# A spectral filter beside a gated feed-forward network on one core: the DRAM scratch of its two turns split by sides, the filters read once and copied within SBUF, and unpadded filter rows

## The chip, the core and the metric

The kernel runs on one core of a Trainium2 chip. The metric is device time in microseconds (us) of one execution; the kernel before takes 204.1 us, the median of three runs (203.77 to 204.25).

The core's engines are TensorE (PE, with its weight loads shown as PEld), VectorE (DVE), ScalarE (ACT), GpSimd (POOL) and SyncE (SP), which here issues every transfer. SBUF is the on-chip memory of 128 partitions, PSUM the memory that TensorE writes.

## The reference, cut to what matters

```python
x = A_x                                    # (1, 2048, 640) bf16
xn = layernorm(x)                          # over the last axis, no scale
X = rfft2(xn.astype(float32))              # over (2048, 640): 2048 x 321 complex
s = irfft2(X * (w_r + 1j * w_i), s=(2048, 640)).astype(bfloat16)
h = (gelu(xn @ w_gate) * (xn @ w_up)) @ w_down    # 640 -> 1536 -> 640, tanh gelu
return x + s * silu(h)
```

`w_r` and `w_i` are 2048 x 321 filters in bf16. Two things are computed from the same normalized rows, then: a two-dimensional spectral filter and a gated feed-forward network.

## The kernel before, in words

**Slabs.** The 2048 rows are split as (n2, n1): slab n1 holds the rows 16 n2 + n1, 128 rows on 128 partitions, and there are 16 slabs (NS = 16). X holds all of them in SBUF.

**The feed-forward network** is the body of the work. For each of four groups of four slabs (g), `ffn_piece` (L714) multiplies the transposed rows xnT by the gate weights into a PSUM bank psg and by the up weights into psu; ACT evicts psg through GELU into ge (L718), and VectorE multiplies psu by ge into uT (L720). `down_third` (L738) then multiplies uT by the down weights, and ACT and VectorE make the silu factor G (L743, L746, L747). psg and psu have two PSUM buffers each.

**The spectral filter** is woven into this. It has these steps:
1. `fold_a`, `fold_b`: sums and differences of the rows' halves (VectorE).
2. `slab_S1`: the 128-point transform of a slab over n2, five matmuls into a PSUM tile pz (L484), which ACT copies into `zbuf` (L486).
3. `group_D`: the transform over the 640 columns for slab 0 alone and then for five groups of three slabs (DF), matmuls into two PSUM tiles pd (L494, L498). ACT, for two halves VectorE, copies them into `zdbuf` (L510), and SP stores them to the DRAM tile ZDR (L512), one transfer for each slab.
4. `load_B2` reads ZDR back with the 16 slabs on partitions (ten transfers, L530): the first turn.
5. `s2_in` and `s2_out`: in eleven bursts the 16-point transform over the slabs (px, L556), its copy xs (ACT, L564), its products with the filters W1 and W2 (VectorE, L568), the way back (pu, L583), its copies (ACT, L589), and stores to the DRAM tile UDR (L592).
6. `load_V` reads UDR back with rows on partitions (ten transfers, L603): the second turn. `gather` (VectorE, L613) collects leftover columns of V into vr.
7. `slab_S1i` (pv, L631; the fifth of its matmuls takes vr), `group_Di` and `group_cs`, `group_Y`: the inverse transforms; `finish` multiplies by G, adds x and stores.

pz, pd, px, pu and pv all come from one PSUM pool, `psB`, with two buffers under one tag.

**GEN.** One SBUF tile, GEN, is cut by hand into scratch. `vt` (index tables) becomes `zdbuf`, two slots for the groups of step 3, and `fv` (angles) becomes `zbuf`, four slots for the slabs of step 2:

```python
zbuf = fv.rearrange("p g l -> p (g l)").bitcast(BF16)[:, 0:4 * D]...
zdbuf = vt.rearrange("p n k -> p (n k)").bitcast(BF16)[:, 0:12 * LP]...
```

The two don't share bytes.

**The filters** lie in W1 and W2 with the partition index 64 hh + 4 k1 + 2 ri + pm. `w_rows` loads them from DRAM; the rows for ri = 0 and ri = 1 are the same, and are read twice, in rows of 321 values (642 B). `w_edge` (POOL, L127) halves the first and last column.

**What sets the order.** A list `back` names the network's pieces in order, and `put(s, ...)` hangs every other step behind piece s; the program is written out in that order, and each engine works its own instructions in order. For groups 1 to 5 the plan puts three slabs' `slab_S1` behind three successive pieces, `group_D` behind the next, and the next group's first `slab_S1` two pieces later. SP works its transfers in order too; a transfer that waits holds up all behind it. Eight semaphores are used by the transfers in turn, and a transfer waits until the eighth before it has landed. All other waits follow from which tiles an instruction reads and writes.

Of the kernel before, what the change touches and what calls it, by code (L numbers as in the profile page):

```python
# [10 lines left out]
BF16 = mybir.dt.bfloat16  # L11
# [3 lines left out]
P = 128  # L15
S = 2048
D = 640
L = 321
LP = 322
# [4 lines left out]
NS = 16  # L24
# [6 lines left out]
@with_exitstack  # L31
def kernel(
    ctx: ExitStack,
    tc: tile.TileContext,
    A_x: bass.AP,
    A_w_r: bass.AP,
    A_w_i: bass.AP,
    B_x: bass.AP,
    B_w_gate: bass.AP,
    B_w_up: bass.AP,  # L40
    B_w_down: bass.AP,
    out: bass.AP,
):

    nc = tc.nc
    x2 = A_x[0]
    xv = x2.rearrange("(n2 n1) d -> n2 n1 d", n1=NS)
    outv = out[0].rearrange("(n2 n1) d -> n1 n2 d", n1=NS)  # L50

    consts = ctx.enter_context(tc.tile_pool(name="consts", bufs=1))
    big = ctx.enter_context(tc.tile_pool(name="big", bufs=1))
    wts = ctx.enter_context(tc.tile_pool(name="wts", bufs=1))
    xg = ctx.enter_context(tc.tile_pool(name="xg", bufs=5))
    work = ctx.enter_context(tc.tile_pool(name="work", bufs=2))
    psA = ctx.enter_context(tc.tile_pool(name="psA", bufs=2, space=bass.MemoryType.PSUM))
    psB = ctx.enter_context(tc.tile_pool(name="psB", bufs=2, space=bass.MemoryType.PSUM))
    dram = ctx.enter_context(tc.tile_pool(name="dscratch", bufs=1, space=bass.MemoryType.DRAM))

    ZDR = dram.tile([2, NS, P, L], BF16)
    UDR = dram.tile([2, NS, P, L], BF16)


    X = big.tile([P, NS, D], BF16, tag="sX")
    Wg = wts.tile([P, 5, F], BF16)
    Wu = wts.tile([P, 5, F], BF16)
    Wd = wts.tile([P, NT, D], BF16)
    W1 = wts.tile([P, 2, NS, LP], BF16)
    W2 = wts.tile([P, 2, NS, LP], BF16)  # L70
    wgv = B_w_gate.rearrange("(c p) f -> p c f", p=P)
    wuv = B_w_up.rearrange("(c p) f -> p c f", p=P)
    with tc.manual_schedule():
        build(nc, locals())


def build(nc, env):
    consts, big, wts, xg, work, psA, psB = (env[k] for k in ("consts", "big", "wts", "xg", "work", "psA", "psB"))
    ZDR, UDR, X, Wg, Wu, Wd, W1, W2 = (env[k] for k in ("ZDR", "UDR", "X", "Wg", "Wu", "Wd", "W1", "W2"))
    xv, outv, wgv, wuv = (env[k] for k in ("xv", "outv", "wgv", "wuv"))  # L80
# [28 lines left out]

    spw = [(WT, src.rearrange("(k1 r) l -> k1 r l", k1=NS)) for WT, src in ((W1, A_w_r), (W2, A_w_i))]  # L110

    def w_rows(i, hh, ri, pm):
        WT, sp = spw[i]
        p0 = hh * 64 + ri * 2 + pm
        for lo in range(2):
            u0 = lo * 32 + hh * 16
            if pm == 0:
                nc.sync.dma_start(out=WT[p0:p0 + 61:4, lo, :, 0:L], in_=sp[:, u0:u0 + 16, :])
            elif u0 == 0:
                nc.sync.dma_start(out=WT[p0:p0 + 61:4, lo, 1:NS, 0:L], in_=sp[:, 127:112:-1, :])  # L120
                nc.sync.dma_start(out=WT[p0:p0 + 61:4, lo, 0, 0:L], in_=sp[:, 64, :])
            else:
                nc.sync.dma_start(out=WT[p0:p0 + 61:4, lo, :, 0:L], in_=sp[:, 128 - u0:112 - u0:-1, :])

    def w_edge(i):
        WT = spw[i][0]
# [30 lines left out]
    def c1(name, dt=FP32):  # L157
        return consts.tile([P, 1], dt, name=name)
# [64 lines left out]
    def bits(name, fields):  # L223
        n = len(fields)
        ti = consts.tile([P, n], INT32, name=name + "i")
        tf = consts.tile([P, n], FP32, name=name)
        for k, (shift, mask) in enumerate(fields):
            nc.vector.tensor_scalar(out=ti[:, k:k + 1], in0=pint, scalar1=shift, scalar2=mask,
                                    op0=ALU.logical_shift_right, op1=ALU.bitwise_and)
        nc.vector.tensor_copy(out=tf, in_=ti)  # L230
        return [tf[:, k:k + 1] for k in range(n)]

    def affine(name, src, a, b):
# [1 line left out]
        nc.vector.tensor_scalar(out=t, in0=src, scalar1=float(a), scalar2=float(b), op0=ALU.mult, op1=ALU.add)  # L235
        return t

    u_f, hi_f, s_f, h_f, pf, n1_f, z_f = bits(
        "pb", [(0, 63), (6, 1), (0, 31), (5, 1), (0, 127), (1, 15), (0, 1)])
    cs_f = h_f  # L240
    e64 = c1("e64")
    nc.vector.tensor_single_scalar(out=e64, in_=pf, scalar=64.0, op=ALU.is_equal)

    def fma(name, src, k, add, dt=FP32):
        t = c1(name, dt)
        nc.vector.scalar_tensor_tensor(out=t, in0=src, scalar=float(k), in1=add, op0=ALU.mult, op1=ALU.add)
        return t
# [3 lines left out]
    nc.vector.tensor_scalar(out=andm, in0=e64, scalar1=-1023.0, scalar2=2047.0, op0=ALU.mult, op1=ALU.add)  # L251
    orm = c1("orm", INT32)
    nc.vector.tensor_scalar(out=orm, in0=e64, scalar1=512.0, scalar2=None, op0=ALU.mult)
    u64 = fma("u64", e64, 64.0, u_f)

    def times(name, src, k, by):
        t = c1(name)
# [246 lines left out]
    def group_D(i):  # L504
        n0, n = DF[i]
        pd = d_group([Zt.pop(n0 + a) for a in range(n)], FT, LH)
        zd = zdbuf[:, i % 2, 0:n]
        for b in range(2):
            ev = nc.vector.tensor_copy if i in (2, 5) and b == 1 else nc.scalar.copy
            ev(out=zd.rearrange("p a c (m b) -> p a c m b", b=2)[:, :, :, :, b], in_=pd[b])  # L510
        for a in range(n):
            nc.sync.dma_start(out=ZDR[:, n0 + a].rearrange("c p l -> p c l"), in_=zd[:, a, :, 0:L])  # L512

    warm_bank = []

# [7 lines left out]

    def load_B2():
        B2 = big.tile([P, NH, L], BF16, tag="sB", name="B2")
        zv = ZDR.rearrange("c n (z a k h) l -> a (c n z) k h l", z=2, a=2, k=2)
        B4 = B2.rearrange("p (k h) l -> p k h l", k=2)
        for h0, h1 in ((0, 3), (3, 6), (6, 9), (9, 12), (12, 16)):
            for lo in range(2):
                nc.sync.dma_start(out=B4[64 * lo:64 * lo + 64, :, h0:h1, :], in_=zv[lo][:, :, h0:h1, :])  # L530
        st_b["B2"] = B2
        sc = X[:, 0:13, :].rearrange("p n d -> p (n d)")
        n_u, n_p = 2 * 3 * L, 2 * 3 * WB
        st_b["p"] = sc[:, 0:4 * n_p].rearrange("p (s q k x) -> p s q k x", s=2, q=2, k=2)
        st_b["u"] = sc[:, 4 * n_p:4 * n_p + 2 * n_u].rearrange("p (s k x) -> p s k x", s=2, k=2)
# [11 lines left out]
    def s2_in(b):  # L547
# [17 lines left out]
        pp = []  # L565
        for q, WT in enumerate((W1, W2)):
            pp.append(wide(st_b["p"][:, b % 2, q]))
            nc.vector.tensor_tensor(out=pp[-1], in0=xs, in1=WT[:, :, h0:h0 + n, l0:l0 + w], op=ALU.mult)  # L568
        st_b[b] = pp

    uv = UDR.rearrange("c n (z a k h) l -> a (c n z) k h l", z=2, a=2, k=2)

    def s2_out(b):
        h0, n, l0, w = BURSTS[b]
        pp = st_b.pop(b)
        pu = psB.tile([P, 2, 512], FP32, tag="b")
        for q, NM in enumerate((N1, N2)):
            for hh in range(2):
                r = slice(64 * hh, 64 * hh + 64)
                for lo in range(2):  # L580
                    for i, j, kind in s2_tiles(b, lo, hh):
                        ps = pu[64 * lo:64 * lo + 64, hh, i * w:j * w].rearrange("p (h l) -> p h l", l=w)
                        nc.tensor.matmul(ps, lhsT=NM[r, kind, 0:64], rhs=pp[q][r, lo, i:j, :],  # L583
                                         start=(q == 0 and i == 0), stop=(q == 1 and j == n))
        us = st_b["u"][:, h0 // 3 % 2, :, 0:n * L].rearrange("p k (h l) -> p k h l", l=L)
        pv = pu[:, :, 0:n * w].rearrange("p k (h l) -> p k h l", l=w)
        for m in range(2):
            c0 = m * LH + l0 // 2
            nc.scalar.copy(out=us[:, :, :, c0:c0 + (w + 1 - m) // 2], in_=pv[:, :, :, m:w:2])  # L589
        if l0 + w == L:  # L590
            for lo in range(2):
                nc.sync.dma_start(out=uv[lo][:, :, h0:h0 + n, :], in_=us[64 * lo:64 * lo + 64, :, :, :])  # L592

    st_c = {}

# [3 lines left out]
    def load_V():  # L599
        V = big.tile([P, NS, 2 * L], BF16, tag="sB", name="Vin")  # L600
        for n0, n in VP:
            for c in range(2):
                nc.sync.dma_start(out=V[:, n0:n0 + n, c * L:c * L + L],  # L603
                                  in_=UDR[c].rearrange("n p l -> p n l")[:, n0:n0 + n, :])
        st_c["V"] = V
        st_c["Y"] = big.tile([P, NS, D], BF16, tag="sX", name="Yall")

# [31 lines left out]

    w1f = W1.rearrange("p k n l -> p (k n l)")  # L640
    vsbuf = w1f[:, 0:4 * D].rearrange("p (s c k) -> p s c k", s=4, c=5)
# [153 lines left out]
    def put(s, *item):  # L795
        plan[s].append(item)
# [57 lines left out]
    for i, (n0, n) in enumerate(DF):  # L854
        a = F0 if i == 0 else F0 + 5 * i - 3
# [8 lines left out]
    for k in range(4):  # L864
        put(32 + 3 * k, slab_T, 8 + k, 2)
        put(65 + 3 * k, slab_T, 12 + k, 2)
    for k in range(16):
        put(8 + k if k < 8 else (32, 35, 38, 41, 44, 44, 47, 47)[k - 8], w_rows, k // 8, k % 8 // 4, k % 2, k % 4 // 2)
    put(40, w_edge, 0)
    put(z_end + 4, w_edge, 1)  # L870
    put(z_end, load_B2)
# [14 lines left out]
    for i, (n0, n) in enumerate(DG):  # L886
        a = vs0 + 15 * i // 2
# [58 lines left out]
```

## Time and profile before

| | |
|---|---|
| median of three runs | 204.1 us (203.77 to 204.25) |
| the profiled execution, whole | 204.42 us |
| its span | 202.6 us, 4209 instructions |
| PE, PEld busy | 195.6 us (97%), 119.8 us (59%) |
| DVE, ACT, POOL busy | 129.3 us (64%), 122.4 us (60%), 33.4 us (16%) |
| granted TensorE clock | 1.0 |
| transfers | 31.77 MB in 43315 packets, 157 GB/s on average |
| packets under 2 KB | 41504 |
| store to ZDR, issue to landing (median) | 5.3 us, 16 of 160.5 KB |
| loads of V, issue to landing (median) | 6.3 us, 6 of 321 KB; 2.9 us, 4 of 160.5 KB |
| filter loads, issue to landing (median) | 7.7 us (w_r) and 6.0 us (w_i), 28 of 160.5 KB |

Busy times are those of each engine in the one profiled execution, and 1.8 us of the whole lie outside the span. In the lines of the trace, "L486" is line 486 of the kernel, `out<-in` are the program's names, "xN" counts instructions, and what stands behind a group in brackets is the engine's idle time before it and what ended it. A line of the timeline begins with its start and its length in us. SPq rows are issues of transfers; the landing comes later.

### The profile page before, as it was taken

Reading aid. Unit: us, or ns where it says so; the run is one execution under the profiler, and the core shown is the slowest. Engines: PE = TensorE matmul, PEld = TensorE weight load, DVE = VectorE, ACT = ScalarE, POOL = GpSimd, SP = SyncE. Lnnn points to the kernel's source line nnn. Section 1 sums busy time; section 2 is a strip of 40 time slices with the busy share of each in tenths; the row PEclk is TensorE's granted clock in tenths of the full one; section 3 lists DMA queues with packets and bytes.
Section 4 is the critical chain, followed back from the end, with each engine's and each line's share of the span. In section 5 each row is a group of like instructions: output and inputs, shape, how many; then the busy total and the mean of one; then the engine's idle time right before and its main releaser. Section 6 shows DMA issues by size and latency. Waiting matters only on the chain.

```text
span 202.6 us, 4209 instructions
## 1 busy us (share of the span) xinstructions
PE 195.6 (97%) x1574; PEld 119.8 (59%) x1589; DVE 129.3 (64%) x340; ACT 122.4 (60%) x208; POOL 33.4 (16%) x61
## 2 busy tenths in 40 slices
PE   7899999999999999999999999999999999999993
PEld 5688854777555555566644333457775555556762
DVE  7886966786488982533576465342358776867672
ACT  2448657857886768423788688425375647476631
POOL 5327779953000200100000000000000000000000
PEclk9999999999999999999999999999999999999999
DMA  5999999899799999729995233569501334224211
GB/s 167 306 297 305 372 310 142 158 147 137 153 170 143 173 174 174 180 43 226 213 228 111 44 97 101 130 164 317 172 0 68 97 102 127 69 92 144 86 69 60
DMA packets 43315, 31.77 MB, mean 157 GB/s; under 512 B 12192, under 2 KB 41504, under 8 KB 43296
## 3 DMA queue, kind: packets, MB, share of 16 engines
q1 hardware_dynamic: 43296, 31.52, 71.4%
q8 instruction: 12, 0.20, 0.4%
q14 instruction: 7, 0.06, 0.1%
HBM read 21.66 MB, written 7.88 MB: 146 GB/s over the span
## 4 chain that ended last, share of the span: by engine, by line
PE 90%; DVE 4%; DMA 2%; issue 1%; POOL 1%; SPq 0%; ACT 0%; DVEq 0%
PE psu L714 25%; PE psg L714 24%; PE psg L738 13%; PE psu L738 12%; PE pd L494 5%; PE pz L484 2%; PE pv L631 2%; PE pu L583 2%; DMA X<-in_A_x_dram 2%; PE px L556 2%; PE pd L498 2%; DVE st L174 1%; DVE uT L720 1%; POOL rst L190 1%; PE pt L326 0%
## 5 line engine op out<-in xcount | busy, mean ns | idle before, releaser
L714 PE MATMUL psu<-xnT,Wu 128*128 128x512 bf16 (+2 forms) x289 | 60.9, 339 | 0.6 <-issue 0.2
L714 PE MATMUL psg<-xnT,Wg 128*128 128x512 bf16 (+2 forms) x286 | 60.4, 338 | 0.9 <-issue 0.5
L720 DVE TENSOR_TENSOR uT<-psu,ge 128x512 bf16<-128x512 f32 (+2 forms) x59 | 34.3, 585 | 29.8 <-PE psu L714 22.5
L718 ACT ACTIVATE ge<-psg 128x512 bf16<-128x512 f32 (+2 forms) x59 | 30.5, 518 | 27.6 <-PE psg L714 25.9
L738 PEld LDWEIGHTS <-uT 128*128 128x128 bf16 x384 | 36.3, 98 | 14.6 <-issue 0.6
L714 PEld LDWEIGHTS <-Wu 128*128 128x128 bf16 x295 | 26.6, 98 | 22.9 <-issue 2.7
L714 PEld LDWEIGHTS <-Wg 128*128 128x128 bf16 x295 | 26.6, 98 | 21.9 <-issue 1.5
L738 PE MATMUL psg<-Wd,uT 128*128 128x320 bf16 (+1 forms) x192 | 30.3, 302 | 0.0
L738 PE MATMUL psu<-Wd,uT 128*128 128x320 bf16 (+1 forms) x192 | 29.2, 296 | 0.0
L568 DVE TENSOR_TENSOR X<-xs,W 128x972 bf16<-128x972 bf16 (+2 forms) x22 | 13.3, 646 | 10.6 <-ACT xs L564 10.6
L174 DVE BATCH_NORM_STATS2 st<-X 128x6 f32<-128x320 bf16 x32 | 14.2, 482 | 0.5 <-DMA X<-in_A_x_dram 0.3
L633 ACT CAST W<-pv 128x640 bf16<-128x640 f32 x16 | 11.1, 692 | 5.4 <-PE pv L631 5.4
L510 ACT CAST GEN<-pd 128x966 bf16<-128x966 f32 (+1 forms) x10 | 10.4, 1102 | 5.3 <-PE pd L498 5.3
L656 ACT ACTIVATE W<-pd 128x960 bf16<-128x960 f32 (+2 forms) x14 | 10.1, 780 | 5.0 <-PE pd L498 5.0
L486 ACT CAST GEN<-pz 128x640 bf16<-128x640 f32 x16 | 11.0, 697 | 3.2 <-PE pz L484 3.2
L589 ACT CAST X<-pu 128x486 bf16<-128x486 f32 (+4 forms) x22 | 12.3, 558 | 0.3
L564 ACT CAST xs<-px 128x972 bf16<-128x972 f32 (+2 forms) x11 | 10.3, 936 | 2.4 <-PE px L556 2.4
L190 POOL TENSOR_TENSOR rst<-ve,mhalf 128x1 f32<-128x1 f32 (+2 forms) x9 | 6.5, 717 | 29.5 <-DVE ve L188 29.5
L662 DVE TENSOR_TENSOR W<-W 128x960 bf16<-128x960 bf16 (+1 forms) x12 | 6.8, 599 | 4.8 <-ACT W L656 4.8
L689 DVE TENSOR_TENSOR Yall<-Yall,G 128x640 bf16<-128x640 bf16 (+3 forms) x18 | 8.1, 450 | 2.1 <-ACT G L743 1.9
L747 DVE SCALAR_TENSOR_TENSOR G<-th,psu 128x320 bf16<-128x320 f32 x8 | 3.9, 488 | 8.4 <-ACT th L746 8.4
L452 DVE TENSOR_TENSOR f<-uvt 128x512 bf16<-128x512 bf16 x16 | 6.7, 421 | 3.0 <-PE pz L484 2.9
(137 smaller groups left out, 202.5 us busy)
## 6 DMA issues: line engine op xcount, KB each, us to landing
ZDR<-GEN SPq DMA_DIRECT2D x16, 160.5 KB, 5.3
xt<-in_A_x_dram SPq DMA_DIRECT2D x8, 320.0 KB, 3.5
UDR<-X SPq DMA_DIRECT2D x10, 240.8 KB, 3.6
W<-in_A_w_r_dram SPq DMA_DIRECT2D x14, 160.5 KB, 7.7
W<-in_A_w_i_dram SPq DMA_DIRECT2D x14, 160.5 KB, 6.0
out_dram<-Yall SPq DMA_DIRECT2D x14, 160.0 KB, 1.8
B<-ZDR SPq DMA_DIRECT2D x8, 240.8 KB, 5.5
Vin<-UDR SPq DMA_DIRECT2D x6, 321.0 KB, 6.3
```

Source lines behind the costliest of these rows:

```text
L174: nc.vector.bn_stats(out=st[:, k, :], in_=X[:, n1, 320 * k:320 * k + 320])
L486: nc.scalar.copy(out=Zt[n1], in_=pz)
L494: nc.tensor.matmul(out[a][g], lhsT=lhs[a][:, g, :], rhs=T[:, g, 0:w], start=(a == 0), stop=False)
L510: ev(out=zd.rearrange("p a c (m b) -> p a c m b", b=2)[:, :, :, :, b], in_=pd[b])
L564: nc.scalar.copy(out=xs, in_=px[:, :, 0:n * w].rearrange("p k (h l) -> p k h l", l=w))
L568: nc.vector.tensor_tensor(out=pp[-1], in0=xs, in1=WT[:, :, h0:h0 + n, l0:l0 + w], op=ALU.mult)
L589: nc.scalar.copy(out=us[:, :, :, c0:c0 + (w + 1 - m) // 2], in_=pv[:, :, :, m:w:2])
L633: nc.scalar.copy(out=vs, in_=pv)
L714: nc.tensor.matmul(ps, lhsT=WT[:, c, t * P:(t + 1) * P], rhs=xnT[g][:, c, c0:c1_], start=(c == 0), stop=(c == 4))
L718: nc.scalar.activation(out=ges[t], in_=ps, func=ACT.Gelu_apprx_tanh)
L720: nc.vector.tensor_tensor(out=uT[g][:, t, c0:c1_], in0=ps, in1=ges[t], op=ALU.mult)
L738: nc.tensor.matmul(ph, lhsT=uT[g][:, t, j * P:(j + 1) * P], rhs=Wd[:, t, c0:c1_], start=(t == 0), stop=(t == NT - 1))
```

## The change

- ZDR and UDR get a leading axis for the side `a` (the low or high half of the 64 frequencies in each half z), so that the B loads and U stores move all 128 partitions of one `hh` where they moved 64 partitions of both. The partition order of the first transform's tables changes with it (`u_f` is now built from `kh_f` and `z_f`), so that the side is the lowest bit of the partition.
- The stores of `group_D` now read every second partition, `zd[a:P:2]`: two for slab 0, four for each group of three slabs (22 in all for 16). The loads of V write every second partition, `V[a:P:2]`: 20 for 10.
- The filters are read once (`w_plus`, `w_minus`), and `w_twin` copies the partitions of ri = 0 to those of ri = 1 within SBUF. A filter row is 321 values long where it was padded to 322, and `w_plus` reads sixteen rows as one run of 5136 values.
- The issues keep to the same list of places: w_r behind pieces 8 to 15 with its copies behind 26 and 27, w_i behind 32 to 41 with its copies behind 47 and 48.

```diff
-    ZDR = dram.tile([2, NS, P, L], BF16)
-    UDR = dram.tile([2, NS, P, L], BF16)
+    ZDR = dram.tile([2, 2, NS, 64, L], BF16)
+    UDR = dram.tile([2, 2, NS, 64, L], BF16)
...
-    W1 = wts.tile([P, 2, NS, LP], BF16)
-    W2 = wts.tile([P, 2, NS, LP], BF16)
+    W1 = wts.tile([P, 2, NS, L], BF16)
+    W2 = wts.tile([P, 2, NS, L], BF16)
...
-    def w_rows(i, hh, ri, pm):
...
+    def w_plus(i, hh, lo):
         WT, sp = spw[i]
-        p0 = hh * 64 + ri * 2 + pm
-        for lo in range(2):
...
+        p0 = hh * 64
+        u0 = lo * 32 + hh * 16
+        nc.sync.dma_start(out=WT[p0:p0 + 61:4, lo].rearrange("p h l -> p (h l)"),
+                          in_=sp[:, u0:u0 + NS, :].rearrange("k h l -> k (h l)"))
+
+    def w_minus(i, hh, lo):
+        WT, sp = spw[i]
+        p0 = hh * 64 + 1
+        u0 = lo * 32 + hh * 16
+        if u0 == 0:
+            nc.sync.dma_start(out=WT[p0:p0 + 61:4, lo, 1:NS, :], in_=sp[:, 127:112:-1, :])
+            nc.sync.dma_start(out=WT[p0:p0 + 61:4, lo, 0, :], in_=sp[:, 64, :])
+        else:
+            nc.sync.dma_start(out=WT[p0:p0 + 61:4, lo, :, :], in_=sp[:, 128 - u0:112 - u0:-1, :])
+
+    def w_twin(i, pm):
+        v = spw[i][0].rearrange("p a h l -> p (a h l)")
+        nc.sync.dma_start(out=v[2 + pm:P:4], in_=v[pm:P:4])
...
-    u_f, hi_f, s_f, h_f, pf, n1_f, z_f = bits(
-        "pb", [(0, 63), (6, 1), (0, 31), (5, 1), (0, 127), (1, 15), (0, 1)])
+    kh_f, hi_f, s_f, h_f, pf, n1_f, z_f = bits(
+        "pb", [(1, 31), (6, 1), (0, 31), (5, 1), (0, 127), (1, 15), (0, 1)])
...
-    u64 = fma("u64", e64, 64.0, u_f)
+    u64 = fma("u64", e64, 64.0, fma("u_f", z_f, 32.0, kh_f))
...
-        for a in range(n):
-            nc.sync.dma_start(out=ZDR[:, n0 + a].rearrange("c p l -> p c l"), in_=zd[:, a, :, 0:L])
+        for a in range(2):
+            if n == 1:
+                nc.sync.dma_start(out=ZDR[a, :, n0].rearrange("c p l -> p c l"), in_=zd[a:P:2, 0, :, 0:L])
+            else:
+                for c in range(2):
+                    nc.sync.dma_start(out=ZDR[a, c, n0:n0 + n].rearrange("n p l -> p n l"),
+                                      in_=zd[a:P:2, :, c, 0:L])
...
-        zv = ZDR.rearrange("c n (z a k h) l -> a (c n z) k h l", z=2, a=2, k=2)
+        zv = ZDR.rearrange("a c n (z k h) l -> (a c n z) k h l", z=2, k=2)
...
-            for lo in range(2):
-                nc.sync.dma_start(out=B4[64 * lo:64 * lo + 64, :, h0:h1, :], in_=zv[lo][:, :, h0:h1, :])
+            for hh in range(2):
+                nc.sync.dma_start(out=B4[:, hh, h0:h1, :], in_=zv[:, hh, h0:h1, :])
...
-            for lo in range(2):
-                nc.sync.dma_start(out=uv[lo][:, :, h0:h0 + n, :], in_=us[64 * lo:64 * lo + 64, :, :, :])
+            for hh in range(2):
+                nc.sync.dma_start(out=uv[:, hh, h0:h0 + n, :], in_=us[:, hh, :, :])
...
-                nc.sync.dma_start(out=V[:, n0:n0 + n, c * L:c * L + L],
-                                  in_=UDR[c].rearrange("n p l -> p n l")[:, n0:n0 + n, :])
+                for a in range(2):
+                    nc.sync.dma_start(out=V[a:P:2, n0:n0 + n, c * L:c * L + L],
+                                      in_=UDR[a, c, n0:n0 + n].rearrange("n p l -> p n l"))
...
-    for k in range(16):
-        put(8 + k if k < 8 else (32, 35, 38, 41, 44, 44, 47, 47)[k - 8], w_rows, k // 8, k % 8 // 4, k % 2, k % 4 // 2)
+    WL = [(hh, lo) for lo in range(2) for hh in range(2)]
+    for i, places in enumerate(((8, 9, 10, 11, 12, 13, 14, 15, 26, 27), (32, 32, 35, 35, 38, 38, 41, 41, 47, 48))):
+        for k in range(4):
+            put(places[2 * k], w_minus, i, *WL[k])
+            put(places[2 * k + 1], w_plus, i, *WL[k ^ 1])
+        for pm in range(2):
+            put(places[8 + pm], w_twin, i, pm)
```

More of the change, by code (lines that the diff above doesn't have):

```diff
@@ L110, in build @@
     spw = [(WT, src.rearrange("(k1 r) l -> k1 r l", k1=NS)) for WT, src in ((W1, A_w_r), (W2, A_w_i))]
-    def w_rows(i, hh, ri, pm):
+    def w_plus(i, hh, lo):
         WT, sp = spw[i]
-        p0 = hh * 64 + ri * 2 + pm
-        for lo in range(2):
[L116 to L123, printed above, removed]
+        p0 = hh * 64
[14 more added lines that the diff above has]
+        nc.sync.dma_start(out=v[2 + pm:P:4], in_=v[pm:P:4])
     def w_edge(i):
@@ L569, in s2_in @@
         st_b[b] = pp
-    uv = UDR.rearrange("c n (z a k h) l -> a (c n z) k h l", z=2, a=2, k=2)
+    uv = UDR.rearrange("a c n (z k h) l -> (a c n z) k h l", z=2, k=2)
     def s2_out(b):
```

## The prediction

> **What bounds the kernel now.** I read the first and fourth parts of the page, then the engines' waits, then the timelines of ACT, SP, DVE and PE around the two turns through DRAM. The profiled execution took 204.42 us, of which the span is 202.6 and 1.8 lies around it; the median of the runs is 204.1. A measurement of this kernel can tell about 0.2% (0.4 us) from no change.
>
> ```profile
> PE 195.6 (97%) x1574; PEld 119.8 (59%) x1589; DVE 129.3 (64%) x340; ACT 122.4 (60%) x208; POOL 33.4 (16%) x61
> ...
> PE 90%; DVE 4%; DMA 2%; issue 1%; POOL 1%; SPq 0%; ACT 0%; DVEq 0%
> ```
> ```profile
> PEld L556 <- DMA UDR<-X: 0.4, 1, 0.4
> ```
>
> PE is busy from 1.2 us to the end, and the chain that ended last is PE but for the first 14 us and the last 2. The second fence, from the engines' waits, is the only one after the start in which PE stands still for a transfer: 0.4 us. So nothing that moves bytes faster can win more than about 0.4 us; the question is what the change can make PE wait for.
>
> **Transfers that get cheaper (at most -0.4 us).** The filters take 18 issues from DRAM and 4 copies in SBUF instead of 36 from DRAM, and fewer, longer rows; the B and U transfers keep their number and bytes and spread over 128 partitions. All of it is hidden now by PE's own work, so I take 0, with -0.4 as the end. Stores to ZDR go from 16 issues to 22 and loads of V from 10 to 20, at about 0.47 us of SP each. SP can bear that: it is the landing that counts. The one added VectorE instruction (u_f, 0.15 us by its neighbours) stands before the first statistics and is covered by the 0.28 us that VectorE idles at 6.0 us for the second slab of x.
>
> **New waits: the first turn.** The build of the changed program lists its instructions with the semaphores each waits for. Counting DMAs up to the awaited values (eight semaphores in turn) gives the transfer behind each. Two rows differ from before in kind (after's line numbers; L494 was L486, L627 was L613):
>
> ```
> L494 TensorCopy GEN<-pz 128x640 [waits DMAHW2_49,DMAHW3_49,DMAHW1_49,DMAHW4_49,PE_49,Activation_49]
> L627 TensorCopy vr<-Vin 128x4x32 [waits DMAHW4_49,DMAHW5_49,DMAHW3_49,DMAHW6_49,DMAHW2_49,DMAHW7_49,DMAHW1_49,DMAHW0_49]
> ```
>
> The first is ACT's copy of a slab's first-transform result into zbuf. Before, it waited for PE and ACT alone, and a group's copy into zdbuf waited for stores two groups old. Now the first such copy after each of groups 0 to 4 waits for all stores that the group *just* issued. zbuf and zdbuf do not overlap, but both lie in GEN, and the stores now read every second partition (`zd[a:P:2]`); I take it that the dependency tracking no longer sees the two apart. ACT works in order, so GELU evictions queue behind the copy, and PE is held at the group's third slab, whose PSUM buffer the waiting copy must free. What lies there now, on ACT and then on PE (the third slab):
>
> ```profile
> 67.41 2.35 ACT L510 CAST GEN<-pd 128x966 bf16<-128x966 f32 x2 [1.36 <-PE pd L498]
> 69.59 0.62 ACT L718 ACTIVATE ge<-psg 128x512 bf16<-128x512 f32 x1
> 70.07 0.73 ACT L486 CAST GEN<-pz 128x640 bf16<-128x640 f32 x1
> ```
> ```profile
> 72.19 0.44 PE L484 MATMUL pz<-Tfwd,f 128*128 128x128 bf16 x5
> ```
>
> The copy starts 0.31 us after the group's eviction ends (69.76). How long do the stores take? The last group's are issued in an idle queue and are the clean case:
>
> ```profile
> L512 SPq DMA_DIRECT2D ZDR<-GEN x3: 359/468/498, 83.8 to 84.7; - x3
> ...
> DMA to landing us min/median/max: 2.9/3.9/4.2
> ```
> ```profile
> 89.00 6.49 SPq L530 DMA_DIRECT2D B<-ZDR  x10
> ```
>
> Their eviction (VectorE) ends at 83.74, and the B loads, which wait for them, go at 89.00: 5.2 us from eviction to landing. Rows and bytes per group stay the same (768 rows of 642 B). Bounds: 4.3 us (four issues, the last after 3 x 0.47, plus 2.9), and about 10 us where filter loads are ahead (group 3: last issue 72.4, landing 7.5 to 7.9 later). Most filter rows go away and the stalls give the queue time to drain, so I take 5.2, and 5.6 for group 1, which still has filter loads just ahead.
>
> Now PE's delay at each transition: put the copy at the landing, run ACT's listed order on with its durations (0.69 a copy, 0.6 a GELU, 0.1 overlap), and see when the third slab's copy lets the next group start, against today.
> - After group 0 (two stores only; 46.51 + 0.5 + 2.8 = 49.85 against 47.12): third copy ends 52.15, PE wanted to go at 50.69: 1.5.
> - Group 1 (54.42 + 5.6 = 60.0 against 56.23; no slack, the copies already ran late behind a table load): 3.75.
> - Group 2 (eviction ends 61.54 on VectorE; 66.74 against 62.64): 69.1 against 66.05: 3.05.
> - Group 3 (74.96 against 70.07): 77.35 against 73.5: 3.85.
> - Group 4 (82.47 against 77.69): 84.84 against 81.1: 3.75.
>
> Sum 15.9 us. With 4.3 it is 11.0. With the landings of today (6.0, 8.8, 10.3 and 8.0 us for groups 1 to 4, and 52.7 for group 0) it is about 30.
>
> **New waits: the second turn.** The second listed row is VectorE's first gather from V. It now waits for the last eight of the V loads, so for all 20; before, for its own two. Its result feeds the fifth matmul of the first slab.
>
> ```profile
> 132.10 7.01 SPq L603 DMA_DIRECT2D Vin<-UDR  x10
> ```
> ```profile
> DMA to landing us min/median/max: 6.7/7.2/7.7
> ```
> ```profile
> 136.45 0.29 DVE L613 COPY vr<-Vin 128x128 bf16<-128x128 bf16 x2
> ```
> ```profile
> 137.97 0.22 PE L631 MATMUL pv<-Tinv,vr 128*128 128x128 bf16 x1
> ```
>
> The second fence is for the last two loads, issued at 136.2 and 138.2: the last lands at 138.2 + 6.7 = 144.9. With twice the issues: eight small ones at 0.47 us (3.8 us, 0.66 MB), then 1.97 MB at the 300 GB/s of these slices (6.6 us), then 2.4 us to land: again 144.9. Gather 0.3 and a semaphore: PE goes on at 145.3 instead of 137.97, so 7.3 us. The least, at the page's best slice (372 GB/s), is about 5; the most, at 240 GB/s, about 9. Later gathers find everything landed.
>
> **Pace after a standstill.** PE does not start at full pace:
>
> ```profile
> 1.17 4.23 PE L520 MATMUL psg<-GEN 128*128 128x256 bf16 x19 [1.17 <-DVE negpi L204]
> ...
> 5.91 0.38 PE L520 MATMUL psg<-GEN 128*128 128x256 bf16 x2
> ```
>
> 19 matmuls take 223 ns each after the idle start, while the two at 5.91 fit in 0.38 us, and later ones of that width run at 109. A standstill that resets this costs half of some 4.2 us, 2.1 us. Today's longest later gap (0.63 us) shows no reset. I charge it once, to the 7 us gap, and nothing to the gaps under 4 us; the ends are 0 and about 10. [...] No run here shows such a gap yet.
>
> **Sum.** 204.4 + 15.9 + 7.3 + 2.1 = 229.7 on the profiled execution's scale, 229 on that of the median. PE has no slack later to give any of it back.
>
> **Rivals.**
> - *VectorE loses its packed rate on unpadded rows* (10%, on top of the above). With rows of 321, odd rows of the filters begin at an odd element. The products (L568) take 663 ns for 972 elements and 496 for 642: 0.51 ns per element. [...] For it: no two-input instruction here reads such rows. Against it: the gather's second block starts at an odd element (289) and takes 222 ns as the even one does, but it has one input. [...]
> - *The queue stays full* (10%). SBUF copies of 2 x 657 KB stand ahead of the stores of groups 0 and 4 on SP, and each waits for its own loads to land, so SP holds stores back; or strided partitions make rows slower. The landings then stay at today's 6 to 10 us and the first turn costs about 30: 243 us.
> - *The waits do not bite* (3%). The filters' 36 transfers fill the queue now. If an emptier queue lands a group before its copy is due, the change costs nothing and shows its 0.4 us: 204, not slower. The point that decides: landing within 1.8 us (group 1) or 0.3 to 0.4 us (groups 3, 4) of the eviction, and V within 4.35 us of its first issue, which is 2.63 MB at 605 GB/s. Against it: the single store at 49.9 took 2.8 us in all, and no slice passes 372 GB/s.
> - The forecast itself has 75%; 2% are left for what I don't see.
>
> **Numbers.** The forecast's own range: 4.3 us landings, 5 us for V and no slow pace give 204.1 + 16 = 220; 6 us landings, 9 us and two slow starts give about 239. The V and pace terms may move against the first turn, so 218 to 239 holds the first case and the alignment case; the full queue and the harmless waits stay outside, with 15% or so. Faster 0.02, same 0.01, slower 0.97.
>
> **What would show it.** In the changed profile: ACT's waits for DMA ZDR on the pz copy, five times, 3 to 5 us each; in PE, five standstills of 1.5 to 4 us between 47 and 100 us, ahead of third slabs; one of about 7 us at the first gather, put down to DMA Vin; the filter products at 660 ns; matmuls at half pace after the long gap. PE's idle time should rise from 7 to about 30 us while its matmul count stays 1574 or so. Wrong if ACT never waits for ZDR, if V lands within 5 us, or if the products take over 1 us.

## The result and the profile after

The changed kernel takes 235.2 us (median of four runs, 233.45 to 238.28) against 203.9 us for the kernel before beside it (four runs, 203.63 to 204.25). The ratio is 1.1504, 95% interval 1.1428 to 1.158; the run of 238.28 us was disturbed and is not in it. The profiled execution took 233.45 us, its span is 231.4, and the sum that I set against it was 229.7.

From the page, busy times and then the chain's shares by engine:

```profile
PE 200.3 (87%) x1574; PEld 121.3 (52%) x1589; DVE 129.8 (56%) x341; ACT 122.1 (53%) x208; POOL 33.3 (14%) x61
...
PE 69%; SPq 8%; DMA 8%; DVE 5%; ACT 5%; issue 3%; POOL 1%; ACTq 0%; DVEq 0%
```

PE is idle for 31.1 us of its span, against 7.0 before, and its share of the chain falls from 90% to 69%. What came in is SP's issuing, transfers and ACT. No engine's busy time grew by more than 0.5 us but PE's, by 4.7 us with the same count of matmuls (its weight loads, by 1.5); 3.6 of it is slower pace by the rows below, and the rest I can't place. PE's waits (engine, line, what ended them: us in total, times, longest) say where it stands still:

```profile
PE pz L492 <- ACT GEN L494: 13.9, 5, 3.7
PE pv L645 <- DVE vr L627: 10.6, 1, 10.6
```

Behind the first stands ACT, behind the second VectorE, each waiting for transfers (their waits):

```profile
ACT GEN L494 <- DMA ZDR<-GEN: 19.4, 5, 5.0
```
```profile
DVE vr L627 <- DMA xt<-in_A_x_dram: 11.8, 1, 11.8
```

The second names xt, loads that have nothing to do with vr; they were issued right after V's and their event is the last before VectorE goes on. The experiments below show that it is V.

**The first turn.** ACT's timeline around group 3, and PE's ahead of the two last third slabs:

```profile
74.42 2.35 ACT L518 CAST GEN<-pd 128x966 bf16<-128x966 f32 x2 [1.29 <-PE pd L506]
76.62 0.61 ACT L732 ACTIVATE ge<-psg 128x512 bf16<-128x512 f32 x1
82.27 0.69 ACT L494 CAST GEN<-pz 128x640 bf16<-128x640 f32 x1 [5.04 <-DMA ZDR<-GEN]
```
```profile
83.01 0.44 PE L492 MATMUL pz<-Tfwd,f 128*128 128x128 bf16 x5 [3.65 <-ACT GEN L494]
83.29 1.87 PE L728 MATMUL psg<-xnT,Wg 128*128 128x512 bf16 x5
84.96 1.83 PE L502 MATMUL pd<-FT,GEN 128*128 128x161 bf16 x12
...
95.94 0.44 PE L492 MATMUL pz<-Tfwd,f 128*128 128x128 bf16 x5 [3.66 <-ACT GEN L494]
96.22 1.24 PE L728 MATMUL psu<-xnT,Wu 128*128 128x512 bf16 x5
97.30 0.92 PE L502 MATMUL pd<-FT,GEN 128*128 128x161 bf16 x8
```

The group's evictions end at 76.77, the GELU at 77.23, and the copy of the next slab into zbuf starts at 82.27, 5.5 us after the evictions. Of two gaps of one length, the one at 83.01 is followed by matmuls at a slower pace (five of 512 columns in 1.87 us), the one at 95.94 is not (1.24 us).

**The second turn.** SP's, VectorE's and PE's timelines:

```profile
147.34 13.12 SPq L617 DMA_DIRECT2D Vin<-UDR  x20
```
```profile
164.37 0.30 DVE L627 COPY vr<-Vin 128x128 bf16<-128x128 bf16 x2 [11.85 <-DMA xt<-in_A_x_dram]
```
```profile
164.72 0.29 PE L645 MATMUL pv<-Tinv,vr 128*128 128x128 bf16 x1 [10.60 <-DVE vr L627]
164.81 2.34 PE L752 MATMUL psu<-Wd,uT 128*128 128x320 bf16 x8
166.94 2.31 PE L752 MATMUL psg<-Wd,uT 128*128 128x320 bf16 x8
```

The issues (nanoseconds of one, min/median/max) and their landings, from the view of that line:

```profile
L617 SPq DMA_DIRECT2D Vin<-UDR x20: 603/614/651, 147.3 to 159.8; - x20
...
DMA to landing us min/median/max: 2.3/2.9/4.2
```

SP is at the twenty issues for 13.1 us, so the wait is mostly issuing. Eight matmuls of 320 columns take 1.25 us in the kernel before (from 138.03 us on, granted clock 1.00) and 2.3 here: 16 of them cost 2.1 us more. In the windows view the granted clock is 0.56 in the 5 us from 164.7 on (the figure before the DMA share and the GB/s):

```profile
164.70:169.70 5.00, 4.97 (x25) 2.99 (x26) 1.06 (x4) 1.26 (x3) 0.00 (x0) 0.56 0.04 12
```

**The filters' products** (groups by form, VectorE) are as fast on rows of 321 as on padded ones, where they took 663 ns:

```profile
L581 DVE TENSOR_TENSOR X<-xs,W 128x972 bf16<-128x972 bf16 x10 | 6.2, 665 | 5.1 <-ACT xs L577 5.1
```

### The profile page after: what moved, and what is told of

Read it like the earlier page. It is cut to its first block, busy times and chain, and to the rows that moved or that the text cites. A ratio compares the mean times of both kernels' runs of the same rounds, so it can differ in the third digit from the quotient of the medians.

```text
span 231.4 us, 4224 instructions
## 1 busy us (share of the span) xinstructions
PE 200.3 (87%) x1574; PEld 121.3 (52%) x1589; DVE 129.8 (56%) x341; ACT 122.1 (53%) x208; POOL 33.3 (14%) x61
## 4 chain that ended last, share of the span: by engine, by line
PE 69%; SPq 8%; DMA 8%; DVE 5%; ACT 5%; issue 3%; POOL 1%; ACTq 0%; DVEq 0%
PE psu L728 17%; PE psg L728 17%; PE psg L752 11%; PE psu L752 10%; DMA ZDR<-GEN 7%; SPq L617 5%; PE pd L502 4%; SPq L524 3%; ACT GEN L518 3%; PE pv L645 2%; PE pu L596 2%; PE pd L506 2%; DMA xt<-in_A_x_dram 2%; PE px L569 2%; ACT GEN L494 2%
## 5 line engine op out<-in xcount | busy, mean ns | idle before, releaser
L728 PE MATMUL psg<-xnT,Wg 128*128 128x512 bf16 (+2 forms) x286 | 60.9, 341 | 0.9 <-issue 0.5
L752 PEld LDWEIGHTS <-uT 128*128 128x128 bf16 x384 | 37.0, 100 | 15.7 <-issue 0.6
L752 PE MATMUL psg<-Wd,uT 128*128 128x320 bf16 (+1 forms) x192 | 31.4, 310 | 0.0
L752 PE MATMUL psu<-Wd,uT 128*128 128x320 bf16 (+1 forms) x192 | 30.3, 303 | 0.0
L494 ACT CAST GEN<-pz 128x640 bf16<-128x640 f32 x16 | 10.7, 703 | 20.1 <-DMA ZDR<-GEN 19.4
L492 PE MATMUL pz<-Tfwd,f 128*128 128x128 bf16 x80 | 7.1, 219 | 13.9 <-ACT GEN L494 13.9
L492 PEld LDWEIGHTS <-f 128*128 128x128 bf16 x80 | 5.8, 97 | 17.8 <-issue 15.2
L518 ACT CAST GEN<-pd 128x966 bf16<-128x966 f32 (+1 forms) x10 | 10.4, 1097 | 6.1 <-PE pd L506 6.1
L645 PE MATMUL pv<-Tinv,vr 128*128 128x128 bf16 x16 | 3.6, 223 | 10.6 <-DVE vr L627 10.6
```

The costliest lines, as they stand in the source:

```text
L492: nc.tensor.matmul(pz[:, c, :], lhsT=chunk(f, n1 % 2, c), rhs=Tfwd[:, n1, :], start=True, stop=True)
L494: nc.scalar.copy(out=Zt[n1], in_=pz)
L728: nc.tensor.matmul(ps, lhsT=WT[:, c, t * P:(t + 1) * P], rhs=xnT[g][:, c, c0:c1_], start=(c == 0), stop=(c == 4))
L752: nc.tensor.matmul(ph, lhsT=uT[g][:, t, j * P:(j + 1) * P], rhs=Wd[:, t, c0:c1_], start=(t == 0), stop=(t == NT - 1))
```

## The experiments

My theory: the strided SBUF sides of the transfers make instructions wait that touch none of the same bytes, once for the stores to ZDR and once for the loads of V; the rest of the change is hidden. The main rival: the transfers themselves, more and smaller, are late. Ten kernels were run. All ratios are to runs of the kernel before on the same chip.

**e1: zbuf in a tile of its own.**

```diff
-    zbuf = fv.rearrange("p g l -> p (g l)").bitcast(BF16)[:, 0:4 * D].rearrange("p (s c k) -> p s c k", s=4, c=5)
+    zbuf = consts.tile([P, 4, 5, P], BF16, name="zbuf")
```

> The changed kernel, with one edit: zbuf, the buffer of the first transform, gets a tile of its own instead of a part of the tile that zdbuf lies in (GEN). The strided stores to ZDR stay. Theory (the copies of pz into zbuf wait for stores that do not touch them): ACT's copy no longer waits for DMA ZDR, the five standstills ahead of the third slabs (16.2 us together, 1.6 of it half pace after one of them) go, the first product matmul of the second stage is back near 93.5 us, the second turn still costs its 10.8 us and its 2.1 us of slow pace; 233.5 - 16.2 = 217.3, so 216 to 220. Rival (strided transfers are slow or the queue is full, and what waits is the real consumer): the standstills move to zdbuf's copies and to the loads of B; 228 to 234.

Measured: 217.66 us, ratio 1.0702 (1.0669 to 1.0735). The stores are the same 22 strided ones, and PE's wait for the copy of pz (L494) is gone from its list. The first matmul of the 16-point transform (px), which marks the end of the first turn, comes at 94.1 us (109.9 in the changed kernel, 93.5 before). The gap ahead of the first inverse slab is still 10.60 us. The rival's standstills ahead of B did not come. Its waits on the copies into zdbuf did: ACT waits 5.9 us there, three times, but PE stands still for them only 0.4 us; e3 and e9 take them up.

**e2: the first two pieces of V in tiles of their own.**

```diff
-        V = big.tile([P, NS, 2 * L], BF16, tag="sB", name="Vin")
+        rest = big.tile([P, NS - 4, 2 * L], BF16, tag="sB", name="Vin")
+        first = [work.tile([P, 2, 2 * L], BF16, tag="xf", bufs=2, name=f"Vfirst{k}") for k in range(2)]
...
-                    nc.sync.dma_start(out=V[a:P:2, n0:n0 + n, c * L:c * L + L],
+                    nc.sync.dma_start(out=T[a:P:2, o:o + n, c * L:c * L + L],
```

> The changed kernel, with one edit: the first two pieces of V (slabs 0 to 3) land in tiles of their own, so that the first gather waits for four loads instead of twenty; the strided loads stay, and the other twelve slabs keep one tile. Theory (the first gather waits for all loads of V because they are strided in one tile): the wait of 10.6 us in PE ahead of the fifth matmul of the first inverse slab goes, no long gap is left there, so the half pace after it (2.1 us) goes too; the first turn keeps its 16.2 us: 233.5 - 10.6 - 2.1 = 220.8, so 220 to 223. If the gap goes and the half pace stays, 222.9. Rival (the loads themselves are late by their twice as many issues): the first gather still waits 4 us or more for its own loads; 225 to 234.

Measured: 221.81 us, ratio 1.089 (1.0849 to 1.0931). The wait of pv is gone from PE's list, though SP issues as before. VectorE's timeline (xt is named at slab 4, which still waits for its whole tile, but PE has work by then):

```profile
154.75 0.29 DVE L633 COPY vr<-Vfirst 128x128 bf16<-128x128 bf16 x2
156.80 0.30 DVE L633 COPY vr<-Vfirst 128x128 bf16<-128x128 bf16 x2
167.16 0.37 DVE L633 COPY vr<-Vin 128x256 bf16<-128x256 bf16 x2 [3.13 <-DMA xt<-in_A_x_dram]
```

The run also shows that the pace after a gap is not decided by the gap's length alone. Its first turn has shorter waits than the changed kernel's (12.4 us in all against 13.9), and yet px starts 2.3 us later, at 112.24: the gaps of 3.21, 3.09 and 2.96 us are each followed by slow matmuls.

```profile
61.03 0.69 PE L492 MATMUL pz<-Tfwd,f 128*128 128x128 bf16 x5 [3.21 <-ACT GEN L494]
61.51 2.34 PE L734 MATMUL psg<-xnT,Wg 128*128 128x512 bf16 x5
```

In the changed kernel a gap of 3.23 us at the same place (61.11) left the pace whole, 1.24 us for the same five.

**e3: both edits together.**

> The changed kernel with both edits: zbuf in a tile of its own, and the first two pieces of V in tiles of their own. Everything else of the change stays: strided stores and loads, filters read once and copied in SBUF, unpadded rows. Theory: the two sets of waits were the whole loss, and the cheaper transfers are hidden: 233.5 - 16.2 - 12.7 = 204.6, so 203.5 to 206, within 1% of the kernel before and not faster by more than 0.4 us. Rival (something else in the change costs time too, such as strided transfers or unpadded rows): 207 to 215. Other rival (transfers on all partitions win something once the waits are gone): under 203.

Measured: 205.38 us, ratio 1.0078 (1.0062 to 1.0094), inside the range, but not nothing. The rest has a name in ACT's waits, on the evictions into zdbuf:

```profile
ACT GEN L518 <- DMA ZDR<-GEN: 8.6, 4, 2.9
```

zdbuf has two slots. Before, an eviction waited only for stores two groups old; here the strided stores of the other slot hold it as well. In the changed kernel this third false wait is covered by that on pz.

**e9: the two slots of zdbuf in a tile each,** zbuf back in GEN, V as in e2.

```diff
-    zdbuf = vt.rearrange("p n k -> p (n k)").bitcast(BF16)[:, 0:12 * LP].rearrange(
-        "p (s a c l) -> p s a c l", s=2, a=3, c=2)
+    zdbuf = [consts.tile([P, 3, 2, LP], BF16, name=f"zdbuf{k}") for k in range(2)]
...
-        zd = zdbuf[:, i % 2, 0:n]
+        zd = zdbuf[i % 2][:, 0:n]
```

> The changed kernel with the two halves of zdbuf in a tile each (zbuf stays in GEN, where no transfer reads it any more), and the first two pieces of V in tiles of their own. In the kernel with both edits before (zbuf moved, the zdbuf halves together) the evictions into one half still waited 8.6 us of ACT's time for the stores of the other half, and the run was 0.8% over the kernel before. Theory (that rest is the same kind of false wait): no more than 1 us of ACT's waits for DMA ZDR on the evictions, first product matmul near 93.6 us instead of 94.9, 203.5 to 204.7. Rival (the rest is the strided transfers or the filters' copies in SBUF): 205 to 206, as without this edit.

Measured: 204.03 us against 203.70, ratio 1.0014 (1.0005 to 1.0023). ACT waits for no transfer any more, the first px starts at 93.61, and the chain is PE again:

```profile
PE 92%; DVE 3%; DMA 2%; POOL 1%; SPq 0%; issue 0%; ACT 0%
```

So the whole change, with the same transfers, costs 0.3 us once its false waits are gone (the interval of the ratio just excludes no change), and wins nothing.

**e10: e9 with the filters' part undone** (padded rows, 36 reads, places of before).

> The kernel of e9 without the filters' part: padded rows and 36 reads of the filters from DRAM at the places of the kernel before; the scratch by sides with B and U on all partitions stays, with zdbuf and V in tiles of their own. Theory (what is left of a loss is the filters' copies in SBUF, which stand ahead of stores; alone they cost 0.33%): 203.3 to 204.2, up to 0.7 us below e9. Rival (the filters' old reads fill the queue, as they did with strided stores, 227.2 against 217.7 or so): 205 to 208.

Measured: 203.98 us, ratio 1.0018 (1.001 to 1.0027), the same as e9. What the filters' part costs alone (e6, below) it does not cost beside the new B and U, and the old reads do no harm where nothing waits falsely.

**e4: in the kernel before, strided stores to ZDR alone.**

```diff
-        for a in range(n):
-            nc.sync.dma_start(out=ZDR[:, n0 + a].rearrange("c p l -> p c l"), in_=zd[:, a, :, 0:L])
+        for a in range(2):
...
+                    nc.sync.dma_start(out=ZDR[c, n0:n0 + n, a:P:2].rearrange("n p l -> p n l"),
+                                      in_=zd[a:P:2, :, c, 0:L])
```

> The kernel before, with one edit: the stores to ZDR read every second partition (22 stores, each of one side, instead of 16); the loads of B keep their form, as do V, U and the filters with their padded rows and 36 reads. Theory (false waits on the store): ACT's copy of pz waits for DMA ZDR after groups 0 to 4. The landings are those of a queue that still carries the filter reads of before, so the loss is at least that of the changed kernel's first turn, 16 us, and up to the 30 us of today's landings: 220 to 234. Rival (the first turn's loss comes from the loads of B on 128 partitions, or from the copies of the filters in SBUF standing ahead of stores): 204 to 208.

Measured: 227.24 us, ratio 1.1134 (1.1087 to 1.1182), 23 us for one line. ACT's timeline has the five waits on the copy of pz; the first comes already after group 0's two stores:

```profile
52.25 1.29 ACT L486 CAST GEN<-pz 128x640 bf16<-128x640 f32 x2 [5.07 <-DMA ZDR<-GEN]
...
87.19 0.69 ACT L486 CAST GEN<-pz 128x640 bf16<-128x640 f32 x1 [4.87 <-DMA ZDR<-GEN]
```

The longer landings that the theory allowed for did not come: after groups 1 to 4 the copy starts 4.9 to 5.3 us after the eviction, no later than in the changed kernel. Only group 0 is worse: its copy starts 5.8 us after the eviction, where the changed kernel's started 3.0 us after it, and PE stands still for 3.56 us where it was 0.79. First px at 116.19, 6.3 us later than in the changed kernel. PE's waits for this copy are 15.2 us against 13.9, which is 1.3 of it; the other 5 us go with pace, since four gaps of 2.88 to 3.56 us are followed by slow matmuls here and one in the changed kernel.

**e8: the same 22 stores, each from a contiguous half of the partitions.** Only the two SBUF slices (and the matching DRAM rows) differ from e4.

```diff
-        for a in range(2):
+        for r in (slice(0, 64), slice(64, P)):
...
-                                      in_=zd[a:P:2, :, c, 0:L])
+                                      in_=zd[r, :, c, 0:L])
```

> The kernel before, with one edit: the same 22 stores to ZDR in number and size, but each reads a contiguous half of the partitions (0 to 63, 64 to 127) instead of every second one. Theory (it is the stride in partitions, not the number of stores or 64 partitions to a store, that makes the copy of pz wait): no wait of ACT for DMA ZDR on that copy, 203.5 to 205. Rival (the added stores and their issues cost the time): 210 to 225.

Measured: 206.05 us, ratio 1.0096 (1.007 to 1.0123). ACT waits for no transfer at all. The number and the size of the stores are not it, then; the stride is worth 21 us. What I had expected at nothing costs 2 us, though, and the run lies above the range: the B loads come late, a real wait. SP is done with the last group's stores at 86.6 us, before at 85.2, and the first px comes at 94.54 after a wait of 0.68 us, before at 93.52 without one.

```profile
PE px L561 <- DMA B<-ZDR: 1.4, 2, 0.7
```

**e5: in the kernel before, strided loads of V alone.**

```diff
-                nc.sync.dma_start(out=V[:, n0:n0 + n, c * L:c * L + L],
-                                  in_=UDR[c].rearrange("n p l -> p n l")[:, n0:n0 + n, :])
+                for a in range(2):
+                    nc.sync.dma_start(out=V[a:P:2, n0:n0 + n, c * L:c * L + L],
+                                      in_=UDR[c, n0:n0 + n, a:P:2].rearrange("n p l -> p n l"))
```

> The kernel before, with one edit: V is loaded by 20 transfers into every second partition instead of by 10 into all; U is stored as before. Theory (the first gather waits for all strided loads of its tile): one wait of 10 to 11 us in PE ahead of the fifth matmul of the first inverse slab, half pace after it: 204.0 + 10.7 + 2.1 = 216.8, so 215 to 218. If my prediction's 0.47 us per issue had held, 204 + 7.3 + 2.1 = 213.4. Rival (V is late because of U's stores on all partitions): 204 to 206.

Measured: 216.95 us, ratio 1.0614 (1.0585 to 1.0642). One gap of 10.23 us and half pace after it. No run loads V by contiguous halves, so that the stride is the cause here too, and not the twenty loads, is taken over from e8:

```profile
147.89 0.29 PE L632 MATMUL pv<-Tinv,vr 128*128 128x128 bf16 x1 [10.23 <-DVE vr L614]
147.97 2.34 PE L739 MATMUL psu<-Wd,uT 128*128 128x320 bf16 x8
```

**e6: in the kernel before, the filters' part alone.**

```diff
-    W1 = wts.tile([P, 2, NS, LP], BF16)
-    W2 = wts.tile([P, 2, NS, LP], BF16)
+    W1 = wts.tile([P, 2, NS, L], BF16)
+    W2 = wts.tile([P, 2, NS, L], BF16)
...
+    def w_twin(i, pm):
+        v = spw[i][0].rearrange("p a h l -> p (a h l)")
+        nc.sync.dma_start(out=v[2 + pm:P:4], in_=v[pm:P:4])
```

> The kernel before, with the part on the filters alone: rows of 321 instead of padded ones, read once from DRAM in 18 transfers, 4 copies in SBUF, at the changed kernel's places; ZDR, B, U and V as before. Theory (hidden work): 204.0 +/- 0.4 us, the products at 660 ns. Rival (VectorE loses its packed rate on odd rows): products over 1 us, 207 to 214. Other rival (the copies in SBUF hold up stores on SP): 205 to 210 with waits for DMA ZDR.

Measured: 204.94 us, ratio 1.0033 (1.0018 to 1.0048). The products take 665 ns, as padded. The time is 0.7 us above that of the kernel before, where I had allowed 0.4. PE waits 0.7 us once for B, which it doesn't before. e9 and e10, whose B loads move 128 partitions, show no wait for B (PE's waits in e9, the chain in e10) and no difference between the two kinds of filters. SP issues the B loads of e6 0.4 us later than before (89.43 against 89.00). Ten loads of 128 partitions take SP 4.64 us in the changed kernel, ten of 64 took 6.49 before. I read that as the old B loads having no room to spare; why they are issued later in e6 was not tried.

**e7: the changed kernel with 48 matmuls added into the long gap.**

```diff
+        if n1 == 0:
+            for _ in range(48):
+                nc.tensor.matmul(pv[:, 0:4, :], lhsT=ident, rhs=Tinv[:, 0:4, :], start=True, stop=True)
```

> The changed kernel with 48 matmuls of 128x512 added ahead of the first inverse slab, whose result is overwritten; they fill the 10.6 us that PE stands still there. Theory (the half pace after the gap comes from PE's standing still): the granted clock stays at 1.00 in the stretch after the gap, its first matmuls of 320 columns take 1.25 us for eight instead of 2.3, and the time falls by up to 2.1 us: 231.3, 231 to 232.5. Rival (the pace is not tied to standing still, or the added matmuls only lengthen PE's work): 233.5 to 236.

Measured: 231.42 us, ratio 1.1338 (1.1308 to 1.1368), with 10.5 us more of matmuls. PE's timeline:

```profile
151.96 10.52 PE L645 MATMUL pv<-Tinv,ident 128*128 128x512 bf16 x48
162.32 0.39 PE L648 MATMUL pv<-Tinv,Vin 128*128 128x128 bf16 x4
163.59 0.23 PE L648 MATMUL pv<-Tinv,vr 128*128 128x128 bf16 x1 [0.88 <-DVE vr L627]
163.65 1.25 PE L755 MATMUL psu<-Wd,uT 128*128 128x320 bf16 x8
164.74 1.25 PE L755 MATMUL psg<-Wd,uT 128*128 128x320 bf16 x8
```

The 16 matmuls that follow take 2.2 us instead of 4.3, and the granted clock there is 1.00, where it was 0.56. So the 2.1 us come from PE standing still. That the profiled run (230.13 us) is 3.3 below that of the changed kernel is not all pace: its vr matmul comes 1.1 us earlier, which is from ahead of the added matmuls.

## Why the prediction was right, and where it was off

The direction and the two causes were right, and the time lay in the range. The terms:

| term | predicted | measured, profiled execution | undone on the chip (difference of ratios x 203.9) |
|---|---|---|---|
| first turn, waits on pz | 15.9 | 16.2, of which about 1.5 is pace | 16.4 (e1) |
| second turn, wait for V | 7.3 | 10.8 | 12.5 with the pace after it (e2) |
| half pace | 2.1, once | 2.1 after V, and the 1.5 above | in e2 and e7 |
| everything else | 0 | 0 | +0.3 (e9) |

204.42 + 16.2 + 10.8 + 2.1 = 233.5 against 233.45. That the first turn comes within 0.3 us of its term is partly luck: without the slow matmuls, which I had at nothing there, it would be 14.7.

- **Transfers that get cheaper win nothing: right.** B's landing went from 5.5 to 4.2 us (median) and U's from 3.6 to 2.5, and e9, which has all of it and no false waits, is not faster.
- **Waits on the first turn: the mechanism right, each within 1.1 us.** Starts of the five groups' matmuls give delays of 0.9, 3.3, 2.7, 4.6 and 4.8 us, where I had 1.5, 3.75, 3.05, 3.85 and 3.75. The landing that I took, 5.2 us after the eviction (5.6 for group 1), came as 5.1 (group 1), 5.4, 5.5 and 5.5. The last two are larger mostly for the slow matmuls after 83.01 (0.6 us on the network's five, 0.8 on the group's own). After group 0 PE stood still 0.8 us and ACT waited 2.3, less than the 1.5 and 3 that I had named as signs.
- **Wait for V: the mechanism right, its size too small by 3.5 us; this is the failed step.** I took 0.47 us for an issue, the price of transfers on 128 partitions, let the bytes set the pace at 300 GB/s, and gave the last load 2.4 us to land: 12.8 us from first issue to last landing. An issue of these 64-partition loads takes 0.61 us. Nineteen of them are 11.6 us, and with 0.9 us between them the last starts 12.5 us after the first, where I had 10.4. It lands up to 4.2 us later, so the gather goes 17.0 us after the first issue. The row that I should have taken stood in the trace: the B loads of before, 64 partitions each, ten in 6.49 us, which I quoted for another purpose. So the shortfall is about half issuing and half the late landing of the last loads (the first six land in 2.3 to 2.7 us). From 154 to 165 us the core moved 238 GB/s, less than the 300 that I had taken, with its DMA engines 0.87 busy; what share the bytes had in the late landing was not tried.
- **Pace: priced right, its count was one short.** A gap of 10.6 us costs 2.1, and e7 shows that PE's idleness is the cause. Gaps of 3 to 4 us were charged nothing, and one of them cost about 1.5 us. Over e2, e4 and the changed kernel, gaps of 2.88 to 3.65 us were followed by slow matmuls eight times; 3.23 and 3.66 were not, nor was any of 2.53 or less. So gaps of about 3 to 3.7 us paid now and then, and what decides it was not shown. From 60.9 to 62.0 us the granted clock is 0.50 in e2, after its gap of 3.21, and 1.00 in the changed kernel, after its 3.23. In the changed kernel's gap of 3.65 it falls 4.4 us after PE's last matmul, when PE is at work again (1.00 from 83.5 to 83.7 us, 0.50 from 83.9 on).
- **Rival "unpadded rows lose the packed rate": fallen.** Products of 665 ns here and in e6, on rows of which every second begins at an odd element, against 663 on the padded ones. That these products have a slower rate to fall to was the author's assumption: no run shows the alignment case that the range was to hold, and the runs showed the same time on both kinds of rows.
- **Rival "the queue stays full": fallen.** The copies started 5.1 to 5.5 us after the evictions of groups 1 to 4, not 6 to 10. e4, which keeps the old reads, shows the same, so it is not an emptier queue that made the difference.
- **Rival "the waits do not bite": fallen.** The landing of groups 3 and 4, 5.5 us after the eviction, would have had to come within 0.4.
- **Not seen:** the third false wait, on the slots of zdbuf (1.3 us in e3, from 205.38 to 204.03 in e9), which the first one hides. The prediction's row for the first inverse slab named DMA Vin; the profile names xt. And the chain of the kernel before leaves PE at 198.2 us, 4.4 before its end and not 2; no term of the sum hangs on that.

## What to carry to other kernels

A transfer that steps over partitions in SBUF can tie together what shares its tile, as here the stores of zdbuf did with zbuf (227.24 us with strided stores in e4, 206.05 with halves in e8): before giving a transfer such a slice, ask what else lies in the tile and who writes or reads it next, and give each buffer a tile of its own, which here turned 1.15 into 1.00 without touching a transfer. Price an issue by a row with the same number of partitions (0.61 us for 64 here, 0.47 for 128), not by the nearest name. And look first at what the bottleneck engine waits for: here PE was 97% busy and stood still 0.4 us for transfers, so cheaper ones could win no more than that, and could lose much.

## What the runs showed of the hardware

The time that SP takes to issue a plain transfer went with how many partitions it touches, not with their stride, and was least for all 128: 0.47 us (median) for stores to ZDR of 128 partitions, 0.61 for both strided (e4) and contiguous (e8) ones of 64; 0.61 for B of 64 and 0.43 for B of 128; 0.60 for U of 64 and 0.38 for U of 128; 0.54 for the filters' copies of 32, and mostly near 0.6 for their reads of 16 (0.52 to 0.97). Two stores of 64 partitions thus take SP 2.6 times as long as one of 128. The shape of the slice changes along with the partitions in these rows, so that the partitions alone decide was not tested. Within the change this cut both ways: it made B and U cheaper to issue, and V and ZDR dearer.
